# HGRN scan with a top-1 mixture of experts: the early scatters lose their memsets, and the written order of all jobs is made anew

## The chip, the cores and the metric

The kernel runs on one core of one Trainium2 chip. The metric is the device time of one execution in microseconds (us). Beside the times there is one profiled execution, from which all rows below are taken. Engines are PE (TensorE), DVE (VectorE), ACT (ScalarE), POOL (GpSimd) and SP (SyncE, which here only issues DMAs); PEld is PE's weight load.

## The reference

```python
# x, f_logit: (4, 5056, 256); 4 * 5056 = 20224 tokens
f = lower_bound + (1 - lower_bound) * sigmoid(f_logit)
for t in range(S):                         # a recurrence along the sequence
    h = f[:, t] * h + (1 - f[:, t]) * x[:, t];  y[:, t] = h
x = y.reshape(20224, 256)
compute = x @ w_skip > 0                   # other tokens pass unchanged
e_idx = argmax(x[compute] @ w_gate)        # one of 8 experts
out[compute] = x + softmax_weight * (relu(x @ w1[e]) @ w2[e])   # 256 -> 1024 -> 256
```

## The kernel before

**Chunks.** The sequence is cut into 20 chunks of 256 time steps (the last has 192), each with 4 batches, so a chunk is 1024 tokens or eight tiles of 128. For chunk c, ACT issues the loads of `z` and `x` and does `tanh` and `affine`; DVE does `mixin` and the `scan`s, two halves for each of two blocks k of 128 features; PE does `score` (router logits), `score_turn` and `turn_out` (transposes to token rows), which ACT evicts into `rows`. DVE then routes: `route0`, `route1`, PE's `route2`, `route3` (the row number of each token in a table in HBM that has a stretch for each expert) and `gates`. POOL writes the token numbers (`number`) and then issues eight `send`s (L485): each is an indirect DMA that scatters 128 rows of 258 floats into the table `dispatched`. SP writes the whole chunk to the output once (`keep`).

**Visits.** A visit takes up to four tiles of one expert through its two matrices. There are 27 of them (VISITS, L46, numbered v0 to v26). SP's `fetch` (L538) reads the tokens from the table, and so waits for the scatters of the chunks that it reads; SP's `load_w` (L554) reads the expert's weights, each matrix in two halves of 512 KB (h is 0 or 1). PE turns the tokens (`turn_in`), then `first` and `second` are the two matrix products; ACT and DVE make the rectified hidden values, DVE's `weigh` multiplies by the gate, and POOL's `put_out` (L694) scatters the result to the output. From v5 on each value is split in a high and a low part, which gives three products for one. Visits v0 to v4 are "whole" and use float32 without a split. The first two, v0 and v1, also don't wait for the table: DVE's `pick` makes a selection matrix and PE's `gather` picks the tokens out of the rows of chunk 0 with it.

**Holds.** A weight load of an early visit may not start when its buffer is free but when DVE has come to a certain place: `hold` (L568) is a DVE memset of one element of the buffer, which the load must wait for. Likewise `late_clear` (L331) is a DVE memset of one element of the tile `zero`, for which SP's `clear` (L334) waits; `clear` writes `zero` into the table's rows ahead of each expert's first.

**Pauses.** Behind each scatter POOL does a memset of part of the first row of `zero` (`pause`, L482). `PACE_C, PACE_V = 6, 5` (L44): behind the sends of chunks 0 to 5 and the outputs of visits v0 to v4 it has 128 elements, behind the later ones 258; the last visit's outputs have none. The memset writes the tile that `clear` reads, so a pause behind `clear` in the program waits until that DMA has read it.

**Order.** The program records 2187 jobs with an engine, needs, a cost and a due time, and `run` (L204) emits them in the sequence of the list `ORDER` (L53), which is written out; cost and due time are not read when it is emitted. Each engine, and each DMA queue with the engine that issues to it, goes through its own jobs in this sequence, so a job that waits holds up all behind it on its engine.

Of the kernel before, what the change touches and what calls it, by code (L numbers as in the profile page):

```python
# [16 lines left out]
P = 128  # L17
# [19 lines left out]
RW = D + 2  # L37
# [6 lines left out]
PACE_C, PACE_V = 6, 5  # L44
# [176 lines left out]
def hgrn_moe(ctx, tc, z_d, x_d, lb_d, wr_d, w1_d, w2_d, out_d, disp_d):  # L221
    nc = tc.nc
    V, A, G, T, SP = nc.vector, nc.scalar, nc.gpsimd, nc.tensor, nc.sync
# [258 lines left out]
    def pause(n=RW):  # L482
        G.memset(zero[0:1, 0:n], 0.0)  # L483
# [12 lines left out]
    NV = len(VISITS)  # L496
# [197 lines left out]
    def put_out(v, s):  # L694
# [5 lines left out]
        if v.get("i", NV) < NV - 1:  # L700
            pause(RW if v["i"] >= PACE_V else P)
# [386 lines left out]
```

## Time and profile before

| | us |
|---|---|
| three runs | 589.35, 594.15, 596.0 (median 594.15) |
| profiled execution, its own time | 589.15 |
| its span, first to last instruction | 587.4 |
| PE busy | 552.8 (94% of the span) |
| DVE, POOL, ACT busy | 460.7, 359.6, 332.3 |
| mean granted clock of PE | 0.991 of full speed |
| DMA moved | 146.74 MB, mean 250 GB/s |

The span is short of the execution's time by 1.75 us. Busy time of PE is that of pipelined instructions whose ends are modelled, so a small gap between two of them doesn't show; what an engine did in a stretch of time is read from the views by stage, which the rows below begin with.

### The profile page before, as it was taken

Reading aid. Unit: us, or ns where it says so; the run is one execution under the profiler, and the core shown is the slowest. Engines: PE = TensorE matmul, PEld = TensorE weight load, DVE = VectorE, ACT = ScalarE, POOL = GpSimd, SP = SyncE. Lnnn points to the kernel's source line nnn. Section 1 sums busy time; section 2 is a strip of 40 time slices with the busy share of each in tenths; the row PEclk is TensorE's granted clock in tenths of the full one; section 3 lists DMA queues with packets and bytes.
Section 4 is the critical chain, followed back from the end, with each engine's and each line's share of the span. In section 5 each row is a group of like instructions: output and inputs, shape, how many; then the busy total and the mean of one; then the engine's idle time right before and its main releaser. Section 6 shows DMA issues by size and latency. Waiting matters only on the chain.

```text
span 587.4 us, 11473 instructions
## 1 busy us (share of the span) xinstructions
PE 552.8 (94%) x4020; PEld 502.1 (85%) x4020; DVE 460.7 (78%) x984; ACT 332.3 (57%) x518; POOL 359.6 (61%) x533
## 2 busy tenths in 40 slices
PE   1589989889999999999999999999999999999995
PEld 0378768779989989899798989899899899999995
DVE  4998789798999999988799878786665754656662
ACT  6756656677685766865745675445345443344441
POOL 3068898878379796685879867847943220532015
PEclk9989999999999999999999999999999999999998
DMA  8989999998899789975678953857494714365312
GB/s 318 391 304 371 335 329 329 353 334 335 288 311 369 256 340 338 346 238 197 221 265 312 335 181 119 284 175 271 147 304 144 214 64 143 117 195 192 110 62 55
DMA packets 39575, 146.74 MB, mean 250 GB/s; under 512 B 9551, under 2 KB 10756, under 8 KB 32472
## 3 DMA queue, kind: packets, MB, share of 16 engines
q1 hardware_dynamic: 21640, 83.85, 41.8%
q10 hardware_dynamic: 6048, 41.58, 20.0%
q0 software_dynamic: 11824, 20.53, 9.9%
q8 instruction: 33, 0.54, 0.4%
q14 instruction: 30, 0.25, 0.1%
HBM read 104.28 MB, written 52.28 MB: 267 GB/s over the span
## 4 chain that ended last, share of the span: by engine, by line
PE 77%; DVE 0%; POOL 0%; POOLq 0%; issue 0%
PE po L686 35%; PE ph L642 33%; PE pt L404 4%; PE px L592 3%; PE pq L382 2%; PE pl L396 0%; DVE w2l L585 0%; POOL out L696 0%; POOLq L721 0%; DVE xin L691 0%; DVE hl L661 0%; PE pr L450 0%; PE pr L449 0%; DVE rows L471 0%
## 5 line engine op out<-in xcount | busy, mean ns | idle before, releaser
L487 POOL DMA_INDIRECT dispatched<-rows,posi x158 | 192.0, 1215 | 92.3 <-issue 28.4
L686 PE MATMUL po<-w2h,hh 128*128 128x256 f32 (+4 forms) x592 | 170.8, 289 | 0.0
L696 POOL DMA_INDIRECT out<-xin x80 | 93.5, 1169 | 124.4 <-DVE xin L691 107.7
L649 ACT ACTIVATE hh<-ph 128x512 fp32r<-128x512 f32 (+6 forms) x164 | 88.5, 546 | 140.7 <-PE ph L642 114.3
L686 PE MATMUL po<-w2h,hl 128*128 128x256 f32 (+4 forms) x592 | 165.9, 280 | 1.4 <-DVE hl L661 1.4
L686 PE MATMUL po<-w2l,hh 128*128 128x256 f32 (+4 forms) x592 | 165.7, 280 | 0.0
L661 DVE SCALAR_TENSOR_TENSOR hl<-ph,hh 128x512 fp32r<-128x512 f32 (+6 forms) x164 | 100.2, 621 | 69.4 <-ACT hh L649 69.2
L642 PE MATMUL ph<-xh,w1h 128*128 128x512 f32 (+8 forms) x352 | 129.2, 367 | 1.0 <-ACT hf L654 0.6
L642 PE MATMUL ph<-xh,w1l 128*128 128x512 f32 (+8 forms) x352 | 124.6, 354 | 0.9 <-DVE w1l L585 0.9
L642 PE MATMUL ph<-xl,w1h 128*128 128x512 f32 (+8 forms) x352 | 124.6, 354 | 0.0
L686 PEld LDWEIGHTS po<-w2h,hl 128*128 128x128 f32 (+4 forms) x592 | 110.2, 186 | 3.0 <-DVE hl L661 1.6
L686 PEld LDWEIGHTS po<-w2h,hh 128*128 128x128 f32 (+4 forms) x592 | 110.1, 186 | 2.2 <-ACT w1h L580 0.4
L686 PEld LDWEIGHTS po<-w2l,hh 128*128 128x128 f32 (+4 forms) x592 | 110.4, 187 | 0.0
L368 DVE TENSOR_TENSOR_SCAN xt<-zt,xt 128x514 f32<-128x514 f32 x76 | 91.6, 1218 | 0.4
L642 PEld LDWEIGHTS ph<-xh,w1h 128*128 128x128 f32 x352 | 66.2, 188 | 10.2 <-issue 2.9
L642 PEld LDWEIGHTS ph<-xl,w1h 128*128 128x128 f32 x352 | 66.1, 188 | 7.4
L642 PEld LDWEIGHTS ph<-xh,w1l 128*128 128x128 f32 x352 | 66.4, 189 | 6.0 <-DVE w1l L585 1.1
L483 POOL MEMSET zero<- 1x258 f32 (+1 forms) x236 | 66.2, 280 | 5.3 <-DMA dispatched<-zero 5.3
L411 ACT ACTIVATE rows<-pt 128x512 f32<-128x512 f32 x79 | 45.9, 596 | 26.3 <-PE pt L404 17.4
L585 DVE TENSOR_TENSOR w1l<-rw,w1h 128x1024 fp32r<-128x1024 f32 x44 | 53.4, 1214 | 0.5 <-ACT w1h L580 0.5
L580 ACT ACTIVATE w1h<-rw 128x1024 fp32r<-128x1024 f32 x44 | 46.5, 1058 | 12.8 <-PE ph L642 7.1
L356 DVE SCALAR_TENSOR_TENSOR xt<-zt,xt 128x1024 f32<-128x1024 f32 (+1 forms) x40 | 48.1, 1204 | 7.0 <-ACT zt L351 5.0
(88 smaller groups left out, 690.6 us busy)
## 6 DMA issues: line engine op xcount, KB each, us to landing
rw<-w SPq DMA_DIRECT2D x88, 512.0 KB, 5.0
out<-rows SPq DMA_DIRECT2D x19, 1032.0 KB, 10.5
zt<-z ACTq DMA_DIRECT2D x18, 1028.0 KB
xt<-x ACTq DMA_DIRECT2D x18, 1028.0 KB, 8.6
xin<-dispatched SPq DMA_DIRECT2D x9, 516.0 KB, 4.9
w1f<-w SPq DMA_DIRECT2D x6, 512.0 KB, 10.3
w2f<-w SPq DMA_DIRECT2D x6, 512.0 KB
dispatched<-rows,posi POOLq DMA_INDIRECT x158, 6.6
```

The lines of the kernel that those rows point to most:

```text
L356: V.scalar_tensor_tensor(out=xv, in0=inner(zt[:, k, cs], c), scalar=1.0, in1=xv, op0=ALU.subtract, op1=ALU.mult)
L368: V.tensor_tensor_scan(out=xt, data0=zt, data1=xt, initial=0.0, op0=ALU.mult, op1=ALU.subtract)
L411: A.activation(st[c]["rows"][:, :nt].rearrange("p (s g) e -> p s g e", s=2)[:, :, g, 0:D], st[c]["pt", g], AF.Copy)
L483: G.memset(zero[0:1, 0:n], 0.0)
L487: si = G.indirect_dma_start(out=disp_d, out_offset=bass.IndirectOffsetOnAxis(ap=posi[:, j:j + 1], axis=0), in_=rows[:, j], in_offset=None, ...
L580: A.activation(hi, v["raw"][h, nm], AF.Copy)
L585: V.tensor_tensor(out=lo, in0=v["raw"][h, nm], in1=v["w"][nm, h][0], op=ALU.subtract)
L642: T.matmul(ph[:, i], a[:, k, cs], b[:, k, :w], start=(n == 0), stop=(n == 5))
L649: A.activation(th, v["hid"][u], AF.Relu)
L661: V.scalar_tensor_tensor(out=tl, in0=ph, scalar=0.0, in1=th, op0=ALU.max, op1=ALU.subtract)
L686: T.matmul(v["po"][p][:R, q], a[:, i, cs], b[:, c], start=(fb == 0 and n == 0 and q == 0), stop=(fb == NFB - 1 and n == len(pairs) - 1), s ...
L696: oi = G.indirect_dma_start(out=out_d, out_offset=bass.IndirectOffsetOnAxis(ap=v["ids"][:R, s, D:D + 1], axis=0), in_=v["xin"][:R, s], in_ ...
```

## The change

The pauses behind the sends of chunks 0 to 5 and behind the outputs of v0 to v4 are left out, 48 and 6 of them; the others stay as they are. `ORDER` is another permutation of the same 2187 jobs: no job is added or removed, and none of the jobs' functions changes but for the pauses.

```diff
 ORDER = [
-    0, 1, 2, 43, 3, 4, 44, 5, 6, 7, 8, 10, 83, 12, 48, 45, 9, 84, 49, 41, 806, 828, 13, 832, 11, 51, 50, 14,
-    123, 46, 804, 53, 805, 829, 19, 807, 15, 47, 85, 16, 17, 25, 18, 27, 20, 86, 52, 28, 23, 21, 24, 29, 22,
...
+    0, 1, 3, 2, 43, 4, 5, 44, 6, 10, 7, 12, 83, 8, 84, 9, 45, 11, 46, 13, 17, 18, 806, 51, 14, 47, 807, 48, 52,
+    19, 15, 54, 123, 16, 88, 25, 20, 41, 828, 27, 42, 49, 832, 28, 833, 23, 85, 50, 829, 21, 86, 29, 22, 854,
...
-    def pause(n=RW):
-        G.memset(zero[0:1, 0:n], 0.0)
+    def pause():
+        G.memset(zero[0:1], 0.0)
...
         no_dep(si, SG[c], SG + ["R", "Z"], "each token has a place of its own, not read before")
-        pause(RW if c >= PACE_C else P)
+        if c >= PACE_C:
+            pause()
...
         no_dep(oi, "O", WG[v["m"] + 1:] + ["O"], "each token's row is written once")
-        if v.get("i", NV) < NV - 1:
-            pause(RW if v["i"] >= PACE_V else P)
+        if PACE_V <= v.get("i", NV) < NV - 1:
+            pause()
```

What the new list does to each engine's own sequence, read from the numbers: PE's 545 jobs move by 2.4 places on average and at most 15, DVE's 676 by 4.1 (39), ACT's 559 by 4.3 (48), POOL's 259 by 4.0 (28), SP's 148 by 1.9 (20). At the start:

| engine | list before | new list |
|---|---|---|
| ACT, its loads | z0 first half, x0 first, z0 second, z1, x0 second, x1 | z0 first, x0 first, x0 second, z0 second, z1, x1 |
| SP, first twelve | w1 of v0 h0, w1 of v1 h0, w2 of v0 h0, w2 of v1 h0, clear, w1 of v1 h1, w2 of v0 h1, keep 0, w1 of v0 h1, w1 of v2 h0, fetch v1, fetch v0 | w2 of v0 h0, clear, w1 of v1 h1, w1 of v1 h0, w2 of v2 h0, w1 of v0 h0, w2 of v1 h0, w2 of v1 h1, w1 of v0 h1, w1 of v2 h0, fetch v1, keep 0 |
| DVE, the hold of v0's first half of w1 | 13th, ahead of the second scan of chunk 1 | 33rd, behind two of the scans of chunk 2 |
| DVE, window v1 and mixin of chunk 3 (block 0) | window 31st, mixin 39th | window 41st, mixin 46th |
| DVE, pick of v1 | 44th | 44th |
| PE, ahead of the first job of v0's `first` | 18 jobs | the same 18, turn_out of chunk 2's fourth pair of tiles and score_turn of chunk 2 |
| PE, last two `first`s of v26 | 3, 1, 2 | 2, 1, 3 |

## Rows read from the trace of the kernel before

**Rows 1.** By stage: from:to and length, busy us (instructions) of each engine, clock, DMA, GB/s

```profile
0.00:40.00 40.00, 18.80 (x120) 13.64 (x124) 31.16 (x110) 25.31 (x33) 12.35 (x49) 0.91 0.88 337
40.00:150.00 110.00, 102.55 (x798) 90.10 (x791) 94.38 (x224) 73.35 (x119) 92.81 (x140) 1.00 0.95 337
150.00:570.00 420.00, 420.00 (x3015) 387.10 (x3014) 329.25 (x641) 231.42 (x363) 245.47 (x336) 1.00 0.67 227
570.00:587.40 17.40, 11.47 (x100) 11.26 (x98) 5.89 (x11) 2.18 (x4) 8.93 (x10) 0.90 0.18 46
```

**Rows 2.** PE's waits, 40 to 160 us: us in total, times, longest

```profile
PE pt L404 <- ACT rows L411: 1.7, 1, 1.7
PE po L686 <- DVE hl L661: 1.4, 1, 1.4
...
PE px L592 <- DMA xin<-dispatched: 0.2, 1, 0.2
```

**Rows 3.** POOL's groups by shape: busy us, mean ns | idle us before, what ended it

```profile
L487 POOL DMA_INDIRECT dispatched<-rows,posi x158 | 192.0, 1215 | 92.3 <-issue 28.4 <-ACT zt L346 19.8 <-ACT hh L649 8.4
...
L483 POOL MEMSET zero<- 1x128 f32 x54 | 10.6, 195 | 5.3 <-DMA dispatched<-zero 5.3
```

**Rows 4.** POOL in order of time: start us, us, instruction [idle before it]

```profile
25.98 1.20 POOL L487 DMA_INDIRECT dispatched<-rows,posi  x1 [19.59 <-ACT zt L346]
32.45 0.20 POOL L483 MEMSET zero<- 1x128 f32 x1 [5.27 <-DMA dispatched<-zero]
33.23 1.11 POOL L487 DMA_INDIRECT dispatched<-rows,posi  x1 [0.58 <-issue]
34.68 1.87 POOL L487 DMA_INDIRECT dispatched<-rows,posi  x1 [0.17 <-issue]
...
114.47 0.97 POOL L487 DMA_INDIRECT dispatched<-rows,posi  x1 [0.17 <-DMA rw<-w]
...
120.06 1.05 POOL L487 DMA_INDIRECT dispatched<-rows,posi  x1 [2.95 <-ACT hh L649]
```

**Rows 5.** Waits of SP's queue, 0 to 150 us: us in total, times, longest

```profile
SPq L549 <- DMA dispatched<-rows,posi: 26.8, 15, 5.2
```

**Rows 6.** DVE in order of time, 17 to 42 us

```profile
17.29 0.06 DVE L575 MEMSET w1f<- 1x1 f32 x1
...
31.69 0.13 DVE L513 SCALAR_TENSOR_TENSOR offi_all<-carr,place 128x1 int32<-128x1 f32 x1
...
32.32 3.46 DVE L368 TENSOR_TENSOR_SCAN xt<-zt,xt 128x514 f32<-128x514 f32 x3
...
38.04 1.22 DVE L356 SCALAR_TENSOR_TENSOR xt<-zt,xt 128x1024 f32<-128x1024 f32 x1
...
39.26 0.17 DVE L455 TENSOR_TENSOR carr<-pr,carr 128x18 f32<-128x18 f32 x1
```

**Rows 7.** PE in order of time, 29 to 43 us

```profile
29.52 3.75 PE L534 MATMUL px<-sel,rows 128*128 128x128 f32 x16 [1.59 <-ACT rows L411]
...
36.12 1.95 PE L534 MATMUL px<-sel,rows 128*128 128x128 f32 x16
37.91 0.60 PE L404 MATMUL pt<-ident,xt 128*128 128x128 f32 x4
...
39.48 1.07 PE L382 MATMUL pq<-xt,wq 128*32 128x256 f32 x16 [0.93 <-DVE carr L455]
40.48 2.05 PE L636 MATMUL ph<-xf,w1f 128*128 128x128 f32 x16
```

**Rows 8.** DMA issues by line: KB each, median us from issue to landing

```profile
w1f<-w SPq DMA_DIRECT2D x6, 512.0 KB, 10.3
```

**Rows 9.** By stage, 25 to 36 us: columns as in the first group

```profile
25.00:30.00 5.00, 1.13 (x6) 0.82 (x6) 4.86 (x10) 4.76 (x7) 1.20 (x1) 0.77 0.92 337
30.00:35.00 5.00, 5.00 (x36) 4.18 (x34) 4.90 (x10) 1.15 (x3) 1.80 (x4) 0.55 0.89 363
34.00:36.00 2.00, 1.48 (x18) 0.61 (x18) 1.78 (x3) 1.15 (x3) 1.83 (x3) 0.87 0.25 95
```

222 rows, old and new, of the table ORDER are left out of this document.

## The prediction, made before the changed kernel was run

> **What bounds the kernel.** I read the profile by stage first, then PE's waits, then POOL and DVE in order of time where the change touches them. By stage [rows 1] PE is busy 420.00 of 420 us from 150 to 570, so in 71% of the span nothing that another engine does earlier can help: there the kernel is PE's own work, and no job is added or taken away. What PE has not done is in three places: 21.2 us idle of the first 40 (40 less 18.80), 7.45 us of the 110 from 40 to 150, and 5.9 us at the end, from 570. A change of order can only win or lose there, and whatever is won before 150 us is kept to the end, since PE has no later idle time in which it would have been made up. In the first 40 us the fullest engine is DVE: 31.16 us of 40 in all, and 4.86 and 4.90 us of 5 from 25 to 35 [rows 9]. From 40 to 150 it is the DMA engines (0.95) with POOL at 92.81 of 110 us. So the question for each part is whether it moves PE's idle time in these stages.
>
> **The memsets.** 54 of 128 elements go, at 195 ns each: 10.6 us of POOL [rows 3]. Behind each stands 0.17 us before the next scatter [rows 4]; no two scatters stand without a memset between them in this stage, so whether that gap stays is not shown. The most that goes is 54 x (0.195 + 0.17) = 19.7 us. In the other direction a scatter that comes straight behind another might last as long as the longest seen, 1.87 us, where memset, gap and mean scatter now make 1.58 (1.215 + 0.365): 54 x 0.29 = 15.7 us lost on POOL. I take the memset alone, -10.6 us, the nearest row, since the gap belongs to the DMA behind it as much as to the memset. None of that is on PE's path: PE's only wait of this stage for rows that came back from the table is 0.2 us [rows 2]. It is SP that waits for scatters, 26.8 us in 15 pieces [rows 5], and behind it in its queue are weight loads that PE is not waiting for either. The cover is the order itself, which puts other chunks' work ahead of a visit; were it gone, SP's longest single wait of 5.2 us would be the price. I count **-0.2 us**.
>
> **The pause behind the first scatter** is a case of its own: it stood 5.27 us until `clear` had been done with the tile [rows 4], so the second scatter began at 33.23, 6.05 us behind the end of the first (27.18). Without it chunk 0's scatters follow at once, and the fetches that wait for them (v1, v0) and what is behind those in SP's queue can go some 6 us sooner. What is late next is POOL's own input: from chunk to chunk it must wait for DVE's gates, as it does at 120.06 with 2.95 us idle. PE uses the fetched rows of v0 and v1 only in `weigh`, as it gathers their tokens by itself: 0 us.
>
> **The start.** DVE's first 52 jobs are the same set in both lists, so chunk 3's scans end no sooner, and I look inside that. Before, PE's score of chunk 2 began at 39.48, having waited 0.93 us for route3 of chunk 1 to read its PSUM tile (the carr row at 39.26) [rows 6, 7]. In the new list a mixin of chunk 3 (1.22 us) no longer stands ahead of that route3, while one more hold (0.06) does; so it comes about 1.1 us sooner, and the score at about 38.4. Then PE does one turn_out of chunk 2 and its score_turn, which the list before has behind `first` of v0. Score to next job took 1.0 us, a turn_out of four transposes takes 0.60 (37.91), the score_turn's two about half of that, 0.3 [rows 7]. That puts `first` at 38.4 + 1.9 = 40.3 against 40.48, with 0.9 us of work done beforehand that was done later; less 0.1 for ACT's copy between score and score_turn: **-1.0 us**. The bounds are 0, as DVE has the same work up to its 52nd job, and -1.8, if the score_turn waits for nothing and the score comes at once. The loads of chunk 0 (x's second half ahead of z's) change no more than which of two inputs of the second mixin is last, 0 us. The SP moves are the rival below.
>
> **The gaps between 40 and 150 us.** The largest rows are 1.7 us for a chunk's evicted rows and 1.4 us for a low part [rows 2]. They are where the written order and the chip disagree by a microsecond or two, and a new order has its own. I find no row that says it has fewer: 0 us, with bounds of -7.45 (all gone) and +7.45 (as many again).
>
> **150 us to the end.** From 150 on PE waits for nothing, and the places of PE's last jobs are the same but for two `first`s of the last visit that change places; POOL's outputs still end behind the last `weigh`. 0 us.
>
> **Sum.** 589.15 - 0.2 - 1.0 = 587.95 for an execution like the profiled one. That one is the shortest of the four shown; the middle of the four (589.15, 589.35, 594.15, 596.0) is 591.75, 2.6 us above it, the median of the three runs 5.0 above. I carry the sum to the middle of the four: **590.5 us**. 1% is 5.9 us, which is about what a measurement of this kernel can tell from no change.
>
> **Rival 1: the gaps close (583).** With POOL 10 to 20 us ahead, rows, buffers and fetches come sooner, and the new order may fit the chip so that PE is dense from 40 us on. For it speaks that POOL is at 84% in that stage; against it that only 0.2 us of PE's 7.45 are put down to the table, and the DMA engines are at 0.95 whatever POOL does. All of it gone gives 590.5 - 7.45 = 583.
>
> **Rival 2: the first visit's weights come late (595.3).** The hold of v0's first half of w1 was at 17.29 us, 23 us ahead of use at 40.48. In the new list it is DVE's 33rd job. Before, the same work ended with the second of three scans at 34.6 (32.32 + 2 x 1.15); less window v1 (31.69 to 32.32) and one scan, which are now behind it, that is 32.8 [rows 6]. The one landing of such a load that the profile has took 10.3 us [rows 8]: 43.1, 2.8 us behind the 40.3 at which PE wants it, with all of PE queued behind. It decides from a landing of 7.5 us on. A wait then also lowers PE's clock: before, 1.13 us of work in the 5 us up to 30 is followed by a clock of 0.55 up to 35 [rows 9], and sixteen gather matmuls took 3.75 us there against 1.95 later [rows 7]. Two more microseconds are a fair price for it: 590.5 + 4.8 = 595.3. For it: five weight halves (this one first of them) are let go between DVE's 31st and 38th job. Against it: DMA was at only 0.25 of its capacity from 34 to 36 us [rows 9], since SP and ACT had nothing issued, so the load may find empty engines; and fewer weights have been asked for ahead of it than before.
>
> **Rival 3: unpaced scatters (598).** If the bound of 1.87 us comes true, POOL falls 15.7 us behind by the time it caught up before (114.47 to 120.06 [rows 4]), fetches of v2 to v5 come later by up to that, and PE takes what the order can't cover; half of it is 590.5 + 7.85 = 598. Against it speaks that scatters of 0.97 us and of 1.87 us both stand behind the same memset, so its length doesn't decide how long a scatter takes. The Trainium skill's page "DMA: Bandwidth & Descriptors" (section "SWDGE vs HWDGE vs iDMA") has a rule that speaks for it: each DMA engine goes round its queues in turn, and software-made and hardware-made DMAs feed different ones. By that rule closer scatters would take turns from the weight and chunk loads; the sum by it would be this rival's, by the rows it is the forecast's, and no row of this trace shows turns within an engine.
>
> **Rival 4: nothing of it arrives (591.75).** The 1.0 us at the start may be lost before DVE's 52nd job, and 0.2 is not to be seen.
>
> **Chances.** The forecast 0.48, rival 1 0.14, rival 2 0.14, rival 3 0.09, rival 4 0.15. The forecast's own range is 586 to 595, from the spread of the four executions (3.3 us to either side of their middle) and the start's bounds. Rivals 2 and 4 lie within 598; below, the range reaches to 584, which takes in most of rival 1; what is left out is about half of rival 3, a part of rival 1 and order misfits larger than those of before: 584 to 598. Faster by over 1% are rival 1 and a tail of the forecast, 0.18. Slower by over 1% are rival 3, a third of rival 2, and misfits elsewhere in the order, 0.18. Within 1%: 0.64.
>
> **What would show it.** Right: second scatter within 2 us of the first; POOL idle, not back to back, before 114 us; score of chunk 2 near 38.4 and `first` of v0 near 40.3 with no wait on a DMA; PE idle from 40 to 150 still between 4 and 11 us; PE full from 150 to 570. Wrong: PE waiting at its first `first` for w1f (rival 2), scatters of a mean above 1.5 us before 114 (rival 3), an idle of under 2 us in 40 to 150 (rival 1), or any stage in which PE's clock falls that was at 1.00 before. The forecast is wrong in its method if PE shows idle time behind 150 us: then the order there matters, which I have counted as nothing.

## The result, and the profile after

| | before | after |
|---|---|---|
| median of the executions, us | 593.38 (20 runs) | 587.32 (20 runs) |
| shortest to longest, us | 589.35 to 599.63 | 585.12 to 592.54 |
| profiled execution, us | 589.15 | 586.96 |
| its span, us | 587.4 | 585.2 |

The ratio of after to before is 0.9917, with a 95% interval of 0.9894 to 0.994: 4.9 us of 593.4 (3.6 to 6.3). The medians hold all executions; the ratio leaves out those that were disturbed. The quotient of the two medians is 0.9898, or 6.1 us. Within 1% was right, but narrowly, as the interval reaches past 0.99; 590.5 us was 3.2 us too long, and the gain of 1.2 us that the prediction saw was a quarter of the one measured.

By stage, columns as in the first group of rows; the last four cut the first two stages finer.

```profile
0.00:40.00 40.00, 20.91 (x144) 14.76 (x145) 32.02 (x117) 26.33 (x34) 15.89 (x49) 1.00 0.94 354
40.00:150.00 110.00, 102.92 (x793) 92.01 (x792) 96.99 (x221) 72.98 (x120) 84.05 (x89) 0.97 0.94 337
150.00:570.00 420.00, 420.00 (x3014) 386.73 (x3013) 326.90 (x642) 231.39 (x363) 238.90 (x334) 1.00 0.66 226
570.00:585.20 15.20, 8.67 (x75) 8.45 (x74) 3.18 (x7) 1.61 (x3) 7.34 (x10) 0.93 0.21 52
...
25.00:30.00 5.00, 5.00 (x30) 2.84 (x28) 4.89 (x14) 3.67 (x6) 2.58 (x3) 1.00 1.03 421
...
40.00:90.00 50.00, 47.35 (x365) 39.91 (x364) 45.08 (x103) 34.14 (x58) 39.01 (x38) 1.00 1.00 363
90.00:150.00 60.00, 55.57 (x431) 52.10 (x430) 51.91 (x119) 38.84 (x63) 45.04 (x52) 0.94 0.89 315
120.00:124.00 4.00, 3.56 (x25) 2.01 (x26) 1.13 (x3) 2.02 (x4) 3.51 (x8) 0.50 1.03 393
```

Beside [rows 1], PE's idle time went from 21.2 to 19.1 us in the first 40, from 7.45 to 7.08 in 40 to 150, stayed at 0 up to 570 and went from 5.9 to 6.5 at the end. Its busy time summed over the stages is 552.5 against 552.8. So of 2.2 us between these two spans, 2.1 are the start, where PE is full from 25 to 30 us at a clock of 1.00 (1.13 us at 0.77 in [rows 9]). The rest of the 4.9 is not in this pair of profiles at all, and that is what the experiments had to find.

POOL by shape, and then in order of time, as in [rows 3, 4]:

```profile
L487 POOL DMA_INDIRECT dispatched<-rows,posi x158 | 183.1, 1159 | 111.8 <-issue 31.5 <-ACT rows L411 22.2 <-DVE hl L662 19.2
L483 POOL MEMSET zero<- 1x258 f32 x182 | 55.4, 304 | 0.0
```

```profile
26.81 1.17 POOL L487 DMA_INDIRECT dispatched<-rows,posi  x1 [20.96 <-ACT rows L411]
28.29 0.98 POOL L487 DMA_INDIRECT dispatched<-rows,posi  x1 [0.30 <-issue]
...
80.25 1.06 POOL L487 DMA_INDIRECT dispatched<-rows,posi  x1 [1.64 <-ACT zt L346]
...
92.25 2.51 POOL L487 DMA_INDIRECT dispatched<-rows,posi  x1 [1.52 <-DVE xin L692]
...
95.07 2.80 POOL L487 DMA_INDIRECT dispatched<-rows,posi  x1 [0.30 <-issue]
...
109.36 0.97 POOL L487 DMA_INDIRECT dispatched<-rows,posi  x1 [0.30 <-issue]
110.64 1.26 POOL L697 DMA_INDIRECT out<-xin  x1 [0.30 <-issue]
...
114.11 0.98 POOL L487 DMA_INDIRECT dispatched<-rows,posi  x1 [1.27 <-ACT rows L411]
```

The 54 short memsets are gone, and the second scatter stands 0.31 us behind the first. But two scatters with nothing between them keep a gap of 0.30 us, where a memset and its gap took 0.195 + 0.17 = 0.365. POOL's pace is nearly what it was, and it still runs up to 111.9 us with two waits of 1.5 and 1.6 us. The last scatter of chunk 5 begins at 109.36 against 114.47 in [rows 4], and 4.9 of these 5.1 us are the earlier second scatter (28.29 against 33.23).

PE in order of time, to set beside [rows 7]:

```profile
36.40 0.18 PE L449 MATMUL pr<-pf,upper 128*128 128x9 bf16 x1 [0.42 <-DVE offi_all L514]
...
36.55 1.07 PE L382 MATMUL pq<-xt,wq 128*32 128x256 f32 x16
37.55 0.66 PE L404 MATMUL pt<-ident,xt 128*128 128x128 f32 x4
38.19 0.44 PE L396 MATMUL pl<-ident,sq 128*128 128x128 f32 x2
38.46 1.95 PE L637 MATMUL ph<-xf,w1f 128*128 128x128 f32 x16
...
116.31 0.60 PE L404 MATMUL pt<-ident,xt 128*128 128x128 f32 x4
120.44 1.43 PE L593 MATMUL px<-ident,xin 120*128 120x120 f32 x6 [3.54 <-DMA xin<-dispatched]
```

The score of chunk 2 (36.55) and v0's `first` (38.46) come 2.9 and 2.0 us earlier than before. At 116.9 there is a new hole: v6's turn_in waits 3.54 us for its fetched rows, and PE's clock is 0.50, the lower level, in the four microseconds behind it. Waits for fetched rows stood at 0.2 us in [rows 2]; now they lead PE's waits from 40 to 160 us, 3.54 us for v6 and 1.38 for v2:

```profile
65.97 0.36 PE L593 MATMUL px<-ident,xin 96*128 96x96 f32 x2 [1.38 <-DMA xin<-dispatched]
```

```profile
PE px L593 <- DMA xin<-dispatched: 4.9, 2, 3.5
PE pq L382 <- DVE carr L455: 0.9, 1, 0.9
PE pr L449 <- DVE pf L442: 0.8, 1, 0.8
```

No evicted rows and no low part are among them, the two largest of before. SP's queue shows when v6's rows were asked for (waits, 0 to 150 us, as in [rows 5], and the fetch of v6 before and after):

```profile
SPq L550 <- DMA dispatched<-rows,posi: 29.2, 12, 7.9
```

```profile
118.56 0.40 SPq L549 DMA_DIRECT2D xin<-dispatched  x1
```

```profile
116.45 0.40 SPq L550 DMA_DIRECT2D xin<-dispatched  x1
```

The longest wait of a fetch for the scatters grew from 5.2 to 7.9 us. It is v6's: chunk 5's last scatter begins at 109.36, and the fetch goes out at 116.45. That is 2.1 us sooner than before (118.56), so the rows did not become later. PE comes to them sooner still: it is free for them at 116.9, and before it turned them at 125.29 without a wait.

### The profile page after: what moved, and what is told of

It reads as the page before. It is cut to its first block, busy times and chain, and to the rows that moved or that the text cites. A ratio compares the mean times of both kernels' runs of the same rounds, so it can differ in the third digit from the quotient of the medians.

```text
span 585.2 us, 11424 instructions
## 1 busy us (share of the span) xinstructions
PE 552.5 (94%) x4020; PEld 502.0 (86%) x4020; DVE 459.1 (78%) x984; ACT 332.3 (57%) x518; POOL 346.2 (59%) x479
## 4 chain that ended last, share of the span: by engine, by line
PE 85%; DVE 7%; DMA 5%; issue 1%; ACT 1%; ACTq 0%; POOLq 0%; POOL 0%; SPq 0%
PE po L687 38%; PE ph L643 34%; PE pt L404 4%; PE px L593 3%; PE pq L382 3%; PE ph L637 2%; DVE xt L368 2%; DMA xin<-dispatched 2%; DVE xt L356 1%; DMA dispatched<-rows,posi 1%; DMA zt<-z 1%; PE pl L396 0%; DVE w1l L586 0%; DVE sel L528 0%; ACT rows L411 0%
## 5 line engine op out<-in xcount | busy, mean ns | idle before, releaser
L487 POOL DMA_INDIRECT dispatched<-rows,posi x158 | 183.1, 1159 | 111.8 <-issue 31.5
L404 PE MATMUL pt<-ident,xt 128*128 128x128 f32 x316 | 49.9, 290 | 16.6 <-DVE xt L368 15.2
L404 PEld LDWEIGHTS pt<-ident,xt 128*128 128x128 f32 x316 | 39.1, 149 | 23.8 <-issue 12.7
L586 DVE TENSOR_TENSOR w2l<-rw,w2h 128x1024 fp32r<-128x1024 f32 x44 | 53.3, 1213 | 5.4 <-ACT w2h L581 5.3
```

What stands on the lines that cost most here:

```text
L404: T.transpose(pt[:, s_, k * P:(k + 1) * P], xt[:, k, at(c, 2 * g + s_):at(c, 2 * g + s_) + P], ident)
L487: si = G.indirect_dma_start(out=disp_d, out_offset=bass.IndirectOffsetOnAxis(ap=posi[:, j:j + 1], axis=0), in_=rows[:, j], in_offset=None, ...
L586: V.tensor_tensor(out=lo, in0=v["raw"][h, nm], in1=v["w"][nm, h][0], op=ALU.subtract)
```

## The experiments

The first four ran on one chip, on which the kernel before took 605.97 us (median, 35 runs); the next four on another (594.27, 17 runs), the last four on a third (593.64, 34 runs). Each ratio is to the kernel before on the same chip; it differs from the quotient of the medians given by up to 0.003. The first question was which part of the change pays: the order or the memsets.

**Order alone.** The new list; every pause stays as it was.

```diff
 ORDER = [
-    0, 1, 2, 43, 3, 4, 44, 5, 6, 7, 8, 10, 83, 12, 48, 45, 9, 84, 49, 41, 806, 828, 13, 832, 11, 51, 50, 14,
+    0, 1, 3, 2, 43, 4, 5, 44, 6, 10, 7, 12, 83, 8, 84, 9, 45, 11, 46, 13, 17, 18, 806, 51, 14, 47, 807, 48, 52,
...
```

> The new order with all 54 short memsets left in. If the order brings the gain: a ratio to the kernel before of 0.990 to 0.994, first product of v0 near 38.5 us and PE's clock at 1.00 from 25 to 40 us. If the memsets bring it (rival): 0.998 to 1.002. POOL's pitch per scatter 0.06 us longer than without memsets (0.195 + 0.17 against a gap of 0.30), so its last scatter of chunk 5 some 3 us later.

Measured: 601.71 us, ratio 0.9946 [0.99, 0.9993]. The new list by itself is faster, if barely clear of no change. Two parts of the expectation failed: PE's clock was 0.67 from 25 to 30 us, and `first` of v0 began at 39.91 and not near 38.5, because score_turn ahead of it waited for ACT's copy:

```profile
39.63 0.44 PE L396 MATMUL pl<-ident,sq 128*128 128x128 f32 x2 [1.64 <-ACT sq L389]
```

The pause of 5.27 us behind the first scatter is gone here too, with the memset in its place: the next scatter starts at 28.15, 0.36 us behind the end of the first, since the list issues `clear` earlier.

**Memsets alone.** The old list; the pauses of the first six chunks and five visits left out.

```diff
-        pause(RW if c >= PACE_C else P)
+        if c >= PACE_C:
+            pause()
...
-        if v.get("i", NV) < NV - 1:
-            pause(RW if v["i"] >= PACE_V else P)
+        if PACE_V <= v.get("i", NV) < NV - 1:
+            pause()
```

> The order before, without the 54 memsets. If the order brings the gain: 0.997 to 1.001, although the second scatter follows the first within 0.5 us instead of 6 us. If the memsets bring it: 0.990 to 0.994. PE's first product of v0 stays at 40.5 us and the clock still falls to half near 28 us on both theories.

Measured: 604.82 us, ratio 0.9981 [0.994, 1.0023]: no effect that can be measured. The second scatter begins at 27.51, 0.30 us behind the first, so the pause of 5.27 us is gone here too.

**All memsets kept, on a tile of their own.** The short ones no longer wait for `clear`.

```diff
+    spare = cp.tile([1, RW], F32, name="spare")
...
-        G.memset(zero[0:1, 0:n], 0.0)
+        G.memset((zero if n == RW else spare)[0:1, 0:n], 0.0)
```

> The order before with all memsets, the 54 short ones on a tile of their own, so that none waits for the zero write. If the price of the pauses was that one wait: the same time as without memsets (within 0.2% of that run). If it was the 54 memsets: the same as the kernel before while the run without memsets is faster. POOL starts its second scatter near 27.6 us.

Measured: 603.89 us, ratio 0.9948 [0.9903, 0.9993]. It takes no memset away, only the pause behind the first scatter, and stands no worse than the kernel without the memsets. Its interval ends just under 1, but memsets alone lost the same pause and shows no gain. The two intervals overlap over most of their length, so no order between the two is shown.

**The new start, then the old order.** No early memsets; the first 172 jobs of the new list (up to PE's score of chunk 3, about 50 us), then the rest in the old order.

```diff
 ORDER = [
+    (the new list's first 172 entries)
+    (the other 2015 in the order of the list before)
 ]
```

> No early memsets; the new order's first 172 jobs (to PE's score of chunk 3, near 50 us), then the other jobs in the order before. If the gain is won at the start: 0.990 to 0.995. If it is won by the order from 50 us on: 0.998 to 1.002, with PE's first product of v0 at 38.5 us all the same and more idle between 50 and 150 us.

Measured: 606.13 us, ratio 1.0029 [0.9991, 1.0067]. No gain is measured. But the profile shows less than half of the 2.1 us at the start: `first` of v0 begins at 39.81, where memsets alone had it at 40.67 on this chip and the changed kernel at 38.46 on its own. The score is at 36.31, as early as in the changed kernel; score_turn then waits for ACT's copy, as in order alone:

```profile
39.54 0.44 PE L396 MATMUL pl<-ident,sq 128*128 128x128 f32 x2 [1.57 <-ACT sq L389]
39.81 1.95 PE L637 MATMUL ph<-xf,w1f 128*128 128x128 f32 x16
```

So this run tests some 0.9 us of start, less than its interval can tell from nothing.

On this first chip the kernels with the old list behind 150 us also lose time there. By stage, 375 to 400 us, memsets alone and then order alone:

```profile
375.00:400.00 25.00, 21.65 (x146) 18.94 (x135) 15.80 (x40) 7.75 (x14) 11.83 (x20) 0.93 0.67 237
```

```profile
375.00:400.00 25.00, 24.78 (x183) 22.65 (x182) 18.73 (x47) 9.21 (x17) 19.48 (x30) 1.00 0.50 158
```

With the old list PE misses 3.35 of 25 us there, with the new one 0.22. The profile of order alone is that of the shortest of its twelve executions (590.33 us, 11 below their median), so it does not show that the new list is spared. That gave the next question: do the longer executions of the kernel before lose their time behind 150 us on the other chips as well?

**The changed kernel again, and the kernel before again, for a second profile of each.** No edit.

> The changed kernel again, beside the others of this job: a ratio of 0.988 to 0.995. If the gain is the order's, it equals that of the order alone with the memsets left in (0.993 by medians) to 0.3%; if removing the memsets adds to it (rival), it is 0.3% or more below that. PE waits 2 to 4 us for the rows of v6 near 117 us and its clock falls to half behind it.

> The kernel before, for a second profile of it. If its longer executions lose their time behind 150 us, this profile shows PE idle by 2 us or more there, as the run of the order before without memsets did (3.35 us from 375 to 400); if only before 150 us (rival), PE is full from 150 to 570 as in its first profile.

Measured: after 588.1 us, ratio 0.9907 [0.9869, 0.9946]. That is 0.4% below order alone (0.9946), which by the expectation speaks for the rival, that the removed memsets add to the order. The two intervals overlap and the chips differ, so this stays open. v6's rows were waited for again, 3.09 us at 119.61.

The profiled execution of before took 595.88 us, one of the long ones, where the first profile had one of the shortest. By stage, the first line from the first profile:

```profile
40.00:90.00 50.00, 46.38 (x353) 38.69 (x346) 41.95 (x98) 32.35 (x53) 44.49 (x69) 1.00 0.98 346
```

```profile
40.00:90.00 50.00, 43.22 (x305) 36.30 (x305) 36.76 (x90) 28.34 (x49) 41.05 (x60) 0.93 0.96 347
75.00:80.00 5.00, 1.14 (x6) 0.80 (x7) 4.35 (x12) 0.60 (x1) 4.57 (x7) 0.73 0.99 365
80.00:85.00 5.00, 5.00 (x19) 4.89 (x19) 3.81 (x5) 0.76 (x2) 4.42 (x7) 0.59 0.98 392
```

Not behind 150, where it idles 0.61 us up to 570, but in 40 to 90: PE is busy for 43.22 us there against 46.38 in the first profile of the same kernel, and its clock is 0.59 in a stretch in which it was 1.00. PE's and then SP's order of time say what came late:

```profile
76.23 0.18 PE L450 MATMUL pr<-pf,ones 128*128 128x9 bf16 x1
79.62 5.07 PE L636 MATMUL ph<-xf,w1f 128*128 128x192 f32 x16 [3.22 <-DMA w1f<-w]
```

```profile
70.00 0.33 SPq L565 DMA_DIRECT2D w2f<-w  x1
70.38 1.42 SPq L565 DMA_DIRECT2D w1f<-w  x1
```

v2's second half of w1 was asked for 6 us ahead of its use, and arrived 9.2 us behind its issue. In the first profile it was issued at 69.86 and used at 76.09 without a wait:

```profile
69.86 0.71 SPq L565 DMA_DIRECT2D w1f<-w  x1
```

```profile
76.09 2.87 PE L636 MATMUL ph<-xf,w1f 128*128 128x192 f32 x16
```

The half's buffer had been let go at 56.62; its load stands behind another on SP, which waits for its own buffer until 69.9 (7.3 us). The new list has the two loads the other way round and issues this one at 62.56. That made a theory to test, below.

**The rest of the new order behind the old start**, the mirror of the fourth kernel: the old list's first 172 jobs, then the new order; no early memsets.

```diff
 ORDER = [
+    (the first 172 entries of the list before)
+    (the other 2015 in the order of the new list)
 ]
```

> No early memsets; the order before for its first 172 jobs (to near 50 us), then the other jobs in the new order: the mirror of the run with the new start. If the gain comes from the order behind 50 us: 0.990 to 0.996, with PE's first product of v0 at 40.6 us as before. If it needs both parts together (rival: the later jobs were put in order for an earlier start): 0.997 to 1.003.

Measured: 588.26 us, ratio 0.9874 [0.9818, 0.993], 5 runs. All of the gain is there without the new start (`first` of v0 at 40.16), though five runs leave the interval wide.

**PE kept busy in the hole at 117.** The changed kernel with 24 extra transposes, whose results are overwritten, ahead of v6's turn_in.

```diff
+        if v.get("i") == 6 and k == 0:
+            for _ in range(24):
+                T.transpose(px[:, 0:P], ident, ident)
```

> The changed kernel with 24 idle transposes (of the identity, into v6's own PSUM tile, overwritten by the real ones) ahead of v6's turn_in, where PE waited 3.54 us for rows and its clock then stood at half for some 7 us. If that half clock costs PE's work: 2 to 3.5 us less than the changed kernel (ratio to the kernel before lower by 0.003 to 0.006), clock 1.00 from 116 to 128. If PE only trades it for later waits (rival): the same as the changed kernel, to 0.2%.

Measured: 588.79 us, ratio 0.9878 [0.9827, 0.993]. The clock stays at 1.00 from 90 to 150. By the medians the kernel is 0.7 us slower than the changed one (588.1), by the ratios 0.3% faster (0.9907), so six runs decide for neither expectation. Its profiled execution (590.74 us) lost time in 40 to 90 (46.14 us busy at a clock of 0.93), so what the half clock at 120 costs remains within the noise.

**The late load issued first.** The kernel before, two neighbouring entries exchanged.

```diff
-    ... 858, 214, 859, 857, 864, ...
+    ... 858, 214, 857, 859, 864, ...
```

> The kernel before with two neighbouring entries of its order exchanged on SP: the load of v2's second half of w1 is issued ahead of that of v2's second half of w2, and no longer stands behind the 5.6 to 7.3 us that SP waits for the latter's buffer. It is issued near 63 us in place of 69.9 to 70.4, 13 us ahead of its use at 76.1 and not 6. Theory (the longer executions of the kernel before are those in which this load lands late): PE has no wait for w1f between 40 and 90 us, its busy time there is 46 us or more in the profile, clock 1.00, and the median falls by 3 to 5 us, to a ratio of 0.991 to 0.995. Rival (the load is late in some executions only by chance, and the DMA engines, which are full, make another transfer late in its place): ratio 0.998 to 1.002, and PE idle in that stage as before at some other wait.

Measured: 594.58 us, ratio 1.0027 [0.9992, 1.0063]. The theory fell. The load goes out at 62.18 and PE waits for no weight in 40 to 90, yet nothing is gained. The profiled execution, the shortest of its twelve (590.7), shows another hole in the same stage; by stage, and PE in order of time:

```profile
40.00:90.00 50.00, 45.88 (x333) 38.52 (x326) 40.18 (x93) 31.83 (x55) 42.61 (x65) 0.97 0.97 343
55.00:60.00 5.00, 2.85 (x19) 2.35 (x17) 3.87 (x14) 2.10 (x4) 4.49 (x7) 1.00 1.02 350
60.00:65.00 5.00, 4.91 (x27) 4.82 (x28) 1.48 (x2) 2.60 (x7) 4.51 (x8) 0.66 0.92 354
```

```profile
60.09 1.09 PE L404 MATMUL pt<-ident,xt 128*128 128x128 f32 x8 [2.25 <-ACT rows L411]
61.02 3.50 PE L636 MATMUL ph<-xf,w1f 128*128 128x128 f32 x16
```

Here it is the evicted rows that are late, the wait of 1.7 us in [rows 2], and `first` behind it runs at the lower clock: 3.50 us for sixteen matmuls that take 1.95 at full clock.

**The load made late again.** The changed kernel with v2's w2 half let go 20 places later on DVE and the two loads in their old sequence.

```diff
-    ... 911, 157, 249, ...
+    ... 911, 858, 859, 857, 157, 249, ...
```

> The changed kernel with the one thing undone: the hold of v2's second half of w2 stands 20 places later on DVE (behind the window of v5, near 69.8 us), and SP loads that half first and w1's second half behind it, as in the kernel before. The w1 load goes out near 70.3 us, 5.5 to 6 us ahead of its use at 75.7 to 76.1. Theory (the late load is what the new order removed): PE waits for w1f or w2f in part of the executions, and the median rises by 3 to 5 us over the changed kernel, a ratio of 0.997 to 1.000 against the kernel before. Rival (the gain is in other places of the order): the ratio stays at 0.988 to 0.992.

Measured: 589.22 us, ratio 0.9941 [0.9903, 0.9979]. The load goes out at 70.08. The ratio lies between the two expectations, and its interval overlaps that of the changed kernel. PE's wait for w1f is 0.3 us in its profile, which is that of the shortest of its twelve executions (584.88 us). Inconclusive.

**Work moved into the hole at 117.** The changed kernel with route2 and route3 of chunk 7 and the score of chunk 8 ahead of v6's turn_in.

```diff
-    ... 303, 280, 974, 969, ...
+    ... 303, 280, 310, 311, 336, 974, 969, ...
```

> The changed kernel with three entries of its order moved ahead of the turn_in of v6, which waits 3.5 us for its fetched rows at 117: PE's route2 of chunk 7 and score of chunk 8, and DVE's route3 of chunk 7 (it must go with them, as PE's next tile waits for it). They are 1.3 us of PE's work at full clock; in the changed kernel the score ran at half clock behind the wait and took 1.94 us. Theory (idle time of PE ahead of 150 us is kept to the end): the wait falls from 3.5 to about 2.2 us, the clock falls for less time, and the kernel gains 1.3 to 2.5 us over the changed one, a ratio of 0.985 to 0.989 against the kernel before. Rival (what PE gains there it waits for at the next weights or rows): the time of the changed kernel, 0.988 to 0.992.

Measured: 586.82 us, ratio 0.9895 [0.9863, 0.9928]: faster than the kernel before, not shown to differ from the changed one (0.9907, on another chip), as the rival had it. PE's waits, 40 to 160 us, and two of them in order of time:

```profile
PE px L593 <- DMA xin<-dispatched: 2.4, 2, 1.5
PE ph L643 <- DVE hl L662: 2.2, 1, 2.2
```

```profile
119.03 0.81 PE L593 MATMUL px<-ident,xin 120*128 120x120 f32 x6 [0.91 <-DMA xin<-dispatched]
...
132.77 0.40 PE L643 MATMUL ph<-xh,w1h 128*128 128x360 f32 x1 [2.20 <-DVE hl L662]
```

The hole shrank as meant, from 3.54 to 0.91 us (the wait of 1.5 is v2's, at 65.97 as in the changed kernel). But a wait of 2.2 us for a low part, which the changed kernel does not have, stands at 132.77, and PE's idle time from 40 to 150 us is 7.03 us against 7.08.

**The new order up to 81 us, then the old.** No early memsets; the new list's first 310 jobs.

```diff
 ORDER = [
+    (the new list's first 310 entries)
+    (the other 1877 in the order of the list before)
 ]
```

> No early memsets; the new order's first 310 jobs (up to second of v2, 81 us on PE), then the old order. It holds the earlier load of v2's second half of w1 and nothing of what the new order does later. Theory (the gain is that load): a ratio of 0.990 to 0.994, PE 46 us or more busy of the 50 from 40 to 90 with clock 1.00. Rival (the gain comes from behind 81 us): 0.997 to 1.001.

Measured: 588.82 us, ratio 0.9924 [0.9891, 0.9957]. Nearly all of the gain is there (0.9917 and 0.9907 with the whole list, on other chips). The second half of the expectation failed, for its profile is at 45.58 us and a clock of 0.97 from 40 to 90, after one long wait for v2's rows:

```profile
67.20 0.55 PE L593 MATMUL px<-ident,xin 96*128 96x96 f32 x2 [2.96 <-DMA xin<-dispatched]
```

## Why the prediction was right, and where its size failed

Within 1% came out right partly by luck: the steps that were worked out make a gain of 0.2%, and the one measured, 0.8% by the ratio and 1.0% by the medians, stands at the edge and comes from a part that was put at nothing. Twenty runs of each kernel told it from no change to within 1.4 us, not to the 5.9 us that the prediction allowed a measurement.

**What the three cut lists say.** The new order up to 172 jobs gives nothing (1.0029), from 172 on it gives all (0.9874), and up to 310 it gives nearly all (0.9924). What the last two share is the order of jobs 173 to 310, from about 50 to 81 us on PE. If the parts of the list add up, that is where the gain comes from. Weak places: the three ran on three chips, the first of them on the slower one, where even the whole new list (with its memsets) gave only 0.9946; no kernel had the new order behind 310 alone; and none of the three has the early memsets, so it is not excluded that part of the gain needs the new order and their absence together. Which of the some 140 jobs it is stays open: the one load that the long execution pointed at is not it by itself.

One wait of that stretch does go with the list. With the old order PE waits near 58 us for evicted rows, 1.7, 1.4 and 2.2 us in the two profiles of before and the one with the loads exchanged, and 1.8 in memsets alone. ACT has stood 2.0 to 2.8 us at the `tanh` ahead of that eviction, waiting for a load of `z` (PE, then ACT, first profile of before):

```profile
59.40 1.09 PE L404 MATMUL pt<-ident,xt 128*128 128x128 f32 x8 [1.69 <-ACT rows L411]
```

```profile
57.80 1.06 ACT L346 ACTIVATE zt<-zt 128x1024 f32<-128x1024 f32 x1 [2.28 <-DMA zt<-z]
```

In the eight profiles with the new order of these jobs that wait is 0.5 us in one and absent in seven; all but one have a wait for v2's rows in its place, 0.8 to 3.0 us. No run alters this wait alone, so its share of the gain is not shown.

**The gaps from 40 to 150 us** were the step that failed, in the prediction's words "I find no row that says it has fewer: 0 us". The row could not say it, because one execution has one set of holes. PE's idle time in 40 to 90, by profile: before 3.62 and 6.78 us, the one with the loads exchanged 4.12; after 2.65 and 2.10, the ones of its order with one thing altered 2.77 (load late) and 2.78 (work moved), the rest of the new order behind the old start 2.40. The two others with the new order there stand higher, 3.86 (extra transposes) and 4.42 (up to 81 us). On the slower chip it is 3.18 with the new list, and 4.94, 5.98 and 9.68 in the three kernels with the old order there. Behind 150 us PE makes up nothing, as the prediction held: on the other chips it idles 0 to 0.6 us from there to 570. But a microsecond won ahead of 150 can go to the next wait ahead of 150, as the work moved into the hole at 117 showed. And a longer hole brings half clock behind it: in the 595.88 us execution PE's busy time is 554.9 us against 552.8, with the same work. Its span is 6.7 us longer than the first profile's; 3.16 of idle time and most of those 2.0 us of busy time lie in 40 to 90.

**The carry to the middle of the executions** failed with it. For an execution like the profiled one the sum was 587.95, and the profiled execution of after took 586.96. The 2.6 us that were added for "the middle of the four" assumed that the new order spreads as far above its profiled execution as the old one does. The old one's median lies 4.2 us above its first profile, the new one's 0.4 above its first and 2.4 above its second (585.73). The middle of the four, 591.75, also lay 1.6 us below the median of twenty. The first profile of before was one of the shortest of the old list's executions, so it hid what the new list removes.

**The start** came 1 us better than forecast: 2.1 us of PE's idle time went, against 1.0 with a bound of 1.8. I had moved the score of chunk 2 with its releaser, route3 of chunk 1. In the new list it does not wait for it: the score begins at 36.55, and DVE reads route3's tile only then:

```profile
36.89 0.17 DVE L455 TENSOR_TENSOR carr<-pr,carr 128x18 f32<-128x18 f32 x1
```

In the medians nothing of the start is to be seen (1.0029 with it alone, and 0.9874 without it), but neither run could show it: the first had only some 0.9 us of it, and the second's interval is 3.3 us wide to either side. Whether the 2.1 us last stays open. That start also varies: the clock in 20 to 30 us was 1.00 in the first profile of after, 0.63 and 0.69 in the second.

**The memsets** were rightly costed at nothing on PE's path (0.9981 [0.994, 1.0023] alone), but on POOL the sum was wrong. I took 10.6 us; the pitch shrank by 0.365 - 0.30 = 0.065 us for each of 54, 3.5 us. The rest went into a longer gap, 0.30 us in place of 0.17, a price that no row of before showed. So POOL did not come to idle before 114 us, as I had it among the signs, save for the two short waits.

**Rival 2**, the late first weights, did not happen. The load of v0's first half of w1 left SP at 32.30 in the changed kernel, within 0.5 us of the 32.8 reckoned, and `first` ran at 38.46 without a wait for it. So it landed within 6.2 us, not the 10.3 of [rows 8], and under the 7.5 at which the rival decides. The mechanism is real all the same: in the long execution of before the same kind of load took 9.2 us, and there it cost 3.2.

**Rival 3**, the unpaced scatters, did not happen either: the 48 scatters of chunks 0 to 5 took 1.24 us on average against 1.22 with the memsets, though single ones reached 2.80. (The mean of 1.159 in POOL's row is that of all 158, 110 of which are paced as before.) The Trainium skill's page "DMA: Bandwidth & Descriptors" (section "SWDGE vs HWDGE vs iDMA") has each engine going round its queues in turn; no run here shows such turns, and the kernel that scatters without pause is no slower. **Rival 1**, the gaps close, had the right stage, but of its two causes the order and not POOL, and too large a size: 4.9 us in all, with 7.08 still idle in the profile. **Rival 4**, nothing, is excluded by the interval.

**The signs** that the prediction named: second scatter within 2 us, right; score of chunk 2 and `first` of v0 near 38.4 and 40.3, both 1.8 us sooner; PE idle between 4 and 11 us, right (7.08); full from 150 to 570, right in both profiles. One sign of "wrong" came true as well: the clock fell to 0.50 at 120 us, where it had been 1.00. Whether it had a price was not decided. And the remark that idle time behind 150 us would overturn the method holds for the slower chip, where the old list lost 3.35 us in 375 to 400.

## What to carry to other kernels

Where a kernel's executions spread by 1% or more, profile a long one as well as a short one before you cost a new order: the holes of the short one are those that the order already covers. To find which stretch of a new order pays, cut the list, new up to a job and old behind it and the reverse, and let the medians decide, with the whole new list beside each cut on the same chip; the wait that looks worst in one profile need not be the one. A hole that is filled by hand may come back elsewhere, so count the whole stage.

## What the runs showed of the hardware

- Two indirect scatters issued back to back keep 0.30 us between them; one behind a memset keeps 0.17 us. A memset of 0.195 us between two scatters therefore costs 0.065 us, not its own length.
- One load of 512 KB on the same queue, issued at 69.9 and 70.4 us in two executions of one kernel, was there within 6.2 us in one and after 9.2 us in the other, with the DMA engines at 0.98 and 0.96 of their time in 40 to 90.
- The same kernel had medians of 593.4, 594.3 and 593.6 us in three sets of runs and of 606.0 on the chip of the first experiments. There ACT and DVE show waits of up to 4.8 us (on the other chips up to 2.7) that the profile puts down to no instruction of the kernel; what they are was not found.
